# Loading and converting the input weights of a GLA + gated SSM kernel by column blocks, with the first group's projection moved into the second group's attention

## Chip, cores, metric

The kernel runs on one core of one Trainium2 chip. The metric is device time in microseconds for one launch; times of several runs are given by their median.

## What is computed

The first part is a gated linear attention over 4 batches, 8 heads, 768 steps and head size 48, in float32. The second part projects the attention's output, runs a linear recurrence, gates it and projects back. The weights `w_in` (384 x 1024), `w_out` (512 x 384) and `A_log` come as float64.

```python
for t in range(S):                       # q, k, v, alpha: (4, 8, 768, 48)
    state = alpha[:, :, t, :, None] * state + np.einsum('bhd,bhe->bhde', k[:, :, t], v[:, :, t])
    y[:, :, t] = np.einsum('bhd,bhde->bhe', q[:, :, t], state)
x = y.transpose(0, 2, 1, 3).reshape(B, S, H * D)          # (4, 768, 384)
val, gate = np.split(x @ w_in, 2, axis=-1)                # 512 columns each
for t in range(S):
    h = exp(A_log)[0] * h + val[:, t, :]
    ys[:, t, :] = h
out = (gate * sigmoid(gate) * ys) @ w_out
```

## The kernel before

**Groups.** Each batch is cut into three groups of 256 steps, so there are 12 groups, numbered m or n. A group has two chunks of 128 steps. The work of a group has two halves: attention (m) and the projection part (n), which runs one group behind.

**Attention.** `natural_alpha` (L551) transposes alpha on PE and ACT copies it into `aT`. `products` (L586) is DVE's chain of running products: `first`, the scan `prod`, the scan `inv`. `natural_qk` (L559) transposes k and q, and its `times` multiplies them by the products into `Z`. That is the form of groups 0 to 2, which are loaded in natural layout in 192-byte packets (`load_natural`, L417); later groups are loaded by `load_raw` (L396) in pieces of 32 partitions and turned by DVE. `scores` (L638) multiplies k and q on PE. `masks` (L648) copies one half of the scores by ACT and masks it on POOL, and masks the other half on DVE. `keys` (L629) transposes k, `state` (L679) adds the chunk's keys times values into a PSUM tile and has ACT copy it to `S_sb`, `values` (L655) and `carried` (L667) build y. `join` (L690) has ACT copy y into `xT` and then issues six small DMAs that move its last rows into place, for groups 0 and 1 from POOL's queue, later from those of SP and ACT.

**Projection.** `project(n, cc)` (L704) computes 128 of the 512 value columns (`pv`) and 128 of the gate columns (`pg`), six matmuls each; `gated` (L717) is a DVE scan over `pv`, a Silu on ACT over `pg` and a product on POOL into `f`. `output` (L728) is 16 matmuls with `w_out`, two ACT copies and two stores from SP. The tiles `pv`, `pg`, `o`, `tn` of alpha, `tp` and the warm-up tile share three PSUM buffers (`ps_mm`).

**Weights.** The float64 bits are loaded as pairs of 32-bit words into `bits_in` and `bits_out`. `load_w_in(half, engine)` (L440) loads one half of the partitions (0 to 63 or 64 to 127) in two DMAs, of 48 and of 16 rows, in 8-KB packets. `convert(i)` (L497) turns words into float32 for 128 value and 128 gate columns of `w_in` (i from 0 to 3) or for two row blocks of `w_out` (i = 4, 5): ACT scales the low words into `wr` (two buffers), DVE does two bit operations on the high words, and POOL adds (it is returned as a function, so that it can be called later).

**Order.** Every engine runs its instructions in the order in which the program text issues them. In the opening the load queue on SP holds, in this order: alpha, k, q of group 0, alpha of 1, v of 0, k and q of 1, the first half of `w_in`, v of 1, `w_out`, then alpha, k, q of group 2. The second half of `w_in` is issued from ACT's queue after `masks(0)`. The attention of groups 0 and 1 is written out (L768 to L832), with all four `convert` calls for `w_in` after `masks(1)` and before `state(1, 0)`. `warm` (L780) issues matmuls whose result nothing reads. Then the loop (L836) has for each n: project and gate four blocks, and between them the attention of n + 1 and the DVE steps (`go`) of group n + 2. For n = 0 there is no attention in it; instead it holds the alpha transposes of group 2 and the two conversions of `w_out`.

## Time and profile before

| | |
|---|---|
| median of 8 runs | 324.01 us (322.45 to 327.69) |
| profiled execution | 327.07 us |
| its span, first to last instruction | 325.3 us |
| PE busy | 294.0 us (90%), mean granted clock 0.961 |
| DVE busy | 227.2 us (70%) |
| POOL busy | 115.6 us (36%) |
| ACT busy | 97.1 us (30%) |
| first matmul of the projection of group 0 | 54.69 us |
| first matmul of the projection of group 1 | 80.96 us |
| first conversion of `w_in` (ACT, behind its last load) | 43.88 us |

Busy shares are means over the whole span. The two rows on the projections divide it into an opening, in which groups 0 and 1 are loaded, the weights come in and the first projection runs, and a loop of eleven rounds. A chain of waits follows the work that ended last back to what released it; a hole in a timeline stands in square brackets, with what ended it.

### The profile page before, as it was taken

What the parts mean: (1) busy time and instruction counts of PE and PEld (TensorE: products, weight loads), DVE (VectorE), ACT (ScalarE), POOL (GpSimd) and SP (SyncE); (2) the same over time, 40 slices, a digit from 0 to 9 for tenths busy, and PEclk for the clock granted to TensorE, in tenths of its full rate; (3) what the DMA queues carried; (4) which work ended last, traced back from release to release, by engine and by line L of the source; (5) the groups of instructions that cost most, each with busy time, mean ns of one, the idle gap of its engine ahead of it and who ended that gap; (6) DMA issues with size and microseconds to landing.
All of it is one profiled execution on the core that took longest, in us unless ns stands there. A gap on an engine that the chain in (4) does not pass through costs nothing.

```text
span 325.3 us, 5980 instructions
## 1 busy us (share of the span) xinstructions
PE 294.0 (90%) x2349; PEld 233.6 (72%) x2349; DVE 227.2 (70%) x244; ACT 97.1 (30%) x200; POOL 115.6 (36%) x109
## 2 busy tenths in 40 slices
PE   3998146969999999999999999999999999999991
PEld 3585145846886887878868878878688688786870
DVE  3857056493896896898998998989979689432110
ACT  4160233421421424224214324241243143221201
POOL 6033327490350610822704216318033054150020
PEclk9999856986999999999999999999999999999999
DMA  9999999951952955927919729559169220100101
GB/s 134 163 158 164 125 262 171 222 73 46 230 103 81 236 82 140 215 39 187 190 37 240 118 81 234 83 146 217 28 171 206 63 50 10 52 2 14 48 5 55
DMA packets 66029, 39.71 MB, mean 122 GB/s; under 512 B 47044, under 2 KB 65096, under 8 KB 65608
## 3 DMA queue, kind: packets, MB, share of 16 engines
q1 hardware_dynamic: 63376, 36.78, 58.7%
q10 hardware_dynamic: 2232, 2.27, 4.3%
q0 software_dynamic: 384, 0.20, 0.5%
q8 instruction: 20, 0.33, 0.5%
q14 instruction: 17, 0.14, 0.2%
HBM read 33.33 MB, written 4.72 MB: 117 GB/s over the span
## 4 chain that ended last, share of the span: by engine, by line
PE 80%; DMA 9%; DVE 3%; POOL 3%; ACT 2%; issue 0%; ACTq 0%; DVEq 0%; POOLq 0%
PE pv L713 21%; PE o L734 20%; PE pg L713 18%; DMA bits_in<-in_moe_w_in_dram 8%; PE sc L645 7%; PE y L664 5%; PE y L675 3%; PE st L685 3%; PE tp L635 2%; DMA a_log<-in_moe_A_log_dram 1%; POOL w_in L515 1%; POOL w_out L515 1%; ACT wr L510 1%; DVE inv L611 1%; DVE prod L599 1%; DVE Z L573 1%
## 5 line engine op out<-in xcount | busy, mean ns | idle before, releaser
L726 POOL TENSOR_TENSOR f<-sg,hh 128x256 f32<-128x256 f32 x48 | 60.6, 1262 | 145.7 <-ACT sg L725 144.2
L713 PE MATMUL pv<-xT,w_in 128*128 128x256 f32 x288 | 73.6, 392 | 0.0
L713 PE MATMUL pg<-xT,w_in 128*128 128x256 f32 x288 | 70.2, 380 | 0.0
L734 PE MATMUL o<-w_out,f 128*128 128x384 f32 x192 | 67.4, 505 | 2.9 <-POOL w_out L515 2.9
L713 PEld LDWEIGHTS pv<-xT,w_in 128*128 128x128 f32 x288 | 53.6, 193 | 12.1 <-issue 2.2
L713 PEld LDWEIGHTS pg<-xT,w_in 128*128 128x128 f32 x288 | 55.0, 191 | 7.6
L734 PEld LDWEIGHTS o<-w_out,f 128*128 128x128 f32 x192 | 37.7, 198 | 28.0 <-POOL w_out L515 3.9
L725 ACT ACTIVATE sg<-pg 128x256 f32<-128x256 f32 x48 | 18.4, 384 | 102.4 <-PE pg L713 89.6
L720 DVE TENSOR_TENSOR_SCAN hh<-a_dec,hh,pv 128x256 f32<-128x256 f32 x32 | 23.5, 733 | 33.5 <-PE pv L713 31.6
L652 POOL TENSOR_TENSOR A<-A,mask 128x512 f32<-128x512 f32 x24 | 30.0, 1269 | 35.1 <-ACT A L651 35.1
L599 DVE TENSOR_TENSOR_SCAN prod<-aT,first 128x1024 f32<-128x1024 f32 x12 | 32.8, 2736 | 0.1
L611 DVE TENSOR_TENSOR_SCAN inv<-aT,last 128x1025 f32<-128x1025 f32 x12 | 29.4, 2450 | 0.4
L738 ACT ACTIVATE o_sb<-o 128x384 f32<-128x384 f32 x24 | 11.8, 491 | 55.2 <-PE o L734 55.2
L645 PE MATMUL sc<-Z 48*128 48x128 f32 x384 | 25.5, 278 | 1.4 <-issue 0.8
L685 PE MATMUL st<-v,ktm 128*64 128x48 f32 x320 | 13.9, 232 | 14.0 <-DMA v<-in_v_dram 10.5
L645 PEld LDWEIGHTS sc<-Z 48*128 48x128 f32 x384 | 22.8, 188 | 5.0 <-issue 3.0
L685 PEld LDWEIGHTS st<-v,ktm 128*64 128x64 f32 x320 | 12.2, 146 | 17.8 <-issue 14.1
L664 PE MATMUL y<-A,v 128*64 128x128 f32 x384 | 24.7, 283 | 0.0
L720 DVE TENSOR_TENSOR_SCAN hh<-a_dec,pv 128x256 f32<-128x256 f32 x16 | 10.9, 681 | 16.4 <-PE pv L713 16.4
L664 PEld LDWEIGHTS y<-A,v 128*64 128x64 f32 x384 | 22.1, 143 | 0.2 <-issue 0.2
L653 DVE TENSOR_TENSOR A<-sc,mask 128x512 f32<-128x512 f32 x24 | 16.6, 691 | 7.9 <-PE sc L645 5.5
L590 DVE STREAM_TRANSPOSE aT<-raw_a 128x1024 f32<-128x1024 f32 x9 | 18.4, 2043 | 0.0
(86 smaller groups left out, 278.0 us busy)
## 6 DMA issues: line engine op xcount, KB each, us to landing
raw_k<-in_k_dram SPq DMA_DIRECT2D x24, 192.0 KB, 5.3
raw_q<-in_q_dram SPq DMA_DIRECT2D x24, 192.0 KB, 6.0
v<-in_v_dram SPq DMA_DIRECT2D x24, 192.0 KB, 4.5
out_dram<-o_sb SPq DMA_DIRECT2D x24, 192.0 KB, 1.9
raw_a<-in_alpha_dram SPq DMA_DIRECT2D x23, 192.0 KB, 4.0
raw_a<-in_alpha_dram SPq DMA_DIRECT2D x18, 176.0 KB, 4.1
raw_k<-in_k_dram SPq DMA_DIRECT2D x18, 176.0 KB, 5.5
raw_q<-in_q_dram SPq DMA_DIRECT2D x18, 176.0 KB, 4.9
```

Of the source, the lines that this page charges most:

```text
L590: nc.vector.transpose(out=to.rearrange("p h (c j) -> p h j c", j=NT), in_=raw_bufs[m % NR][name].rearrange("p h (j d) -> p h j d", d=D)[:, ...
L599: nc.vector.tensor_tensor_scan(out=prod, data0=aT[:, 0:4 * GC], data1=first.rearrange("p h n -> p (h n)"), initial=0.0, op0=ALU.mult, op1= ...
L611: nc.vector.tensor_tensor_scan(out=inv[:, ::-1], data0=aT[:, ::-1], data1=last.rearrange("p h n -> p (h n)")[:, 0:4 * GC + 1][:, ::-1], in ...
L645: nc.tensor.matmul(sc[i][:, p, :], Z[rows, p, 1, cols], Z[rows, p, 0, cols], start=True, stop=True)
L652: nc.gpsimd.tensor_mul(A[:, 1], A[:, 1], mb)
L664: nc.tensor.matmul(ys[m][i][ds(64 * s, 64), e, ds(c * C, C)], v_sb[:, c, 2 * p + i, :], A[:, i, p, :], start=(c == 0 and e == 0), stop=Fal ...
L685: nc.tensor.matmul(st[ds(64 * i, 64), p, :], ktms[c][:, p, i, :], vs[m % NV][:, c, 2 * p + i, 0:D], start=(ch == 0 and p == 0), stop=(ch = ...
L713: nc.tensor.matmul(pj, w_in[:, kk, vg, ds(cc * C, C)], xT[:, kk, :], start=(kk == 0), stop=(kk == NK - 1))
L720: nc.vector.tensor_tensor_scan(out=hh, data0=a_dec[:, cc:cc + 1].to_broadcast([C, GC]), data1=pv, initial=prev_h[cc][:, GC - 1:GC] if g el ...
L725: nc.scalar.activation(sg, pg, AF.Silu)
L726: nc.gpsimd.tensor_mul(fs[n][:, cc, :], sg, hh)
L734: nc.tensor.matmul(os[c], fs[n][:, cc, ds(c * C, C)], w_out[:, cc, :], start=(cc == 0), stop=(cc == NI - 1))
```

## The change

`load_w_in` now takes a block number i: it loads the 128 value and the 128 gate columns that `convert(i)` needs, for both halves of the partitions, in eight DMAs of 48 or 16 rows with packets of 1 KB. All four blocks are issued from SP, after v of group 1. `wr` has four buffers. `convert(0)` stands before `scores(1)`, `convert(1)` after `keys(1)`, `convert(2)` before `join(1)`, `convert(3)` before the second block of the projection; `masks(1)` stands ahead of `keys(1)`. Block 0 of the projection of group 0 runs between `convert(1)` and `state(1, 0)`, the other three after `join(1)`, and with them the round n = 0 leaves the loop and is written out. In the start, the Exp table is loaded by a first small activation, three warm calls and the alpha transposes come ahead of the transpose of `a_log`, and the Silu table is loaded after `scores(0)`.

```diff
--- before.py
+++ after.py
@@ -385,6 +385,7 @@
     p1 = pool("p1", 1)
     p2 = pool("p2", 2)
     p3 = pool("p3", 3)
+    p4 = pool("p4", 4)
     ps_sc = pool("ps_sc", 2, space=PS)
     ps_st = pool("ps_st", 1, space=PS)
     ps_mm = pool("ps_mm", 3, space=PS)
@@ -437,12 +438,18 @@
     bits_in = const.tile([C, NK, 2 * DI, 2], U32, name="bits_in")
     bits_out = const.tile([C, NI, DM, 2], U32, name="bits_out")
 
-    def load_w_in(half, engine):
-
-        for row, size, first, step in ((64 * half, D, 4 * half * D, D), (64 * half + D, R, (4 * half + 3) * D, R)):
-            engine.dma_start(out=bits_in[ds(row, size)].rearrange("p kk n two -> p kk (n two)"),
-                             in_=moe_w_in.bitcast(U32)[ds(first, NK * step)]
-                             .rearrange("(kk p) n -> p kk n", p=step)[0:size])
+    def load_w_in(i, engine):
+
+        for first_row, size in ((0, D), (D, R)):
+            for vg in range(2):
+                for s in range(2):
+                    row, step = (4 * s * D, D) if size == D else ((4 * s + 3) * D, R)
+                    cols = ds(2 * (vg * DI + i * C), 2 * C)
+                    engine.dma_start(
+                        out=bits_in[ds(64 * s + first_row, size), :, ds(vg * DI + i * C, C)]
+                        .rearrange("p kk n two -> p kk (n two)"),
+                        in_=moe_w_in.bitcast(U32)[ds(row, NK * step), cols]
+                        .rearrange("(kk p) n -> p kk n", p=step)[0:size])
 
     def load_w_out(i, engine):
         engine.dma_start(out=bits_out[:, ds(2 * i, 2)].rearrange("p cc n two -> p cc (n two)"),
@@ -505,7 +512,7 @@
             bits, w = bits_out[:, rows, None], w_out[:, rows, None, :]
         lo, hi = bits[..., 0], bits[..., 1]
         _, x, y, z = w.shape
-        r = p2.tile([C, x, y, z], I32, tag="wr", name="wr")
+        r = p4.tile([C, x, y, z], I32, tag="wr", name="wr")
         t = w.bitcast(U32)
         nc.scalar.activation(r, lo, AF.Copy, scale=2.0 ** -29)
         nc.vector.tensor_scalar(out=t, in0=hi, scalar1=3, scalar2=0x3FFFFFFF,
@@ -693,9 +700,12 @@
         xT = xTs[m] = p2.tile([C, 4, GC], FP32, tag="xT", name="xT")
         nc.scalar.activation(xT[:, 1::2], y[1], AF.Copy)
         nc.scalar.activation(xT[:, 0::2], y[0], AF.Copy)
-        for s in range(2):
-            for a in range(NK):
-                engines[s].dma_start(out=xT[ds(64 * s + D, R), a], in_=xT[ds(64 * s + R * a, R), 3])
+
+        def transfers():
+            for s in range(2):
+                for a in range(NK):
+                    engines[s].dma_start(out=xT[ds(64 * s + D, R), a], in_=xT[ds(64 * s + R * a, R), 3])
+        return transfers
 
 
     prev_h = [None] * NI
@@ -758,30 +768,31 @@
     load_v(0, SP)
     pair("k", 1, SP, SP)
     pair("q", 1, SP, SP)
-    load_w_in(0, SP)
     load_v(1, SP)
+    for i in range(NI):
+        load_w_in(i, SP)
     for i in range(2):
         load_w_out(i, SP)
 
     constants()
-
+    def warm(count):
+
+        t = ps_mm.tile([C, 4, C], FP32, tag="mm", name="warm")
+        for _ in range(count):
+            nc.tensor.matmul(t, ident, ident[:, None, :].to_broadcast([C, 4, C]), start=True, stop=True)
+
+    nc.scalar.activation(ok[:, 0:1], minus, AF.Exp)
+    warm(3)
+
+
+    natural_alpha(0)
     al = ps_mm.tile([C, NI], FP32, tag="mm", name="al")
     nc.tensor.transpose(al, a_log, ident[0:NI, 0:NI])
     nc.scalar.activation(a_dec, al, AF.Exp)
-    nc.scalar.activation(ok, start_p, AF.Silu)
-
-
-    natural_alpha(0)
     check_alpha(0)
     k_times, q_times = natural_qk(0, "k"), natural_qk(0, "q")
     for name in "akq":
         pair(name, 2, SP, SP)
-
-    def warm(count):
-
-        t = ps_mm.tile([C, 4, C], FP32, tag="mm", name="warm")
-        for _ in range(count):
-            nc.tensor.matmul(t, ident, ident[:, None, :].to_broadcast([C, 4, C]), start=True, stop=True)
 
     warm(5)
     for _ in products(0):
@@ -791,9 +802,9 @@
         q_times(c)
     for c in range(G):
         scores(0, c)
+    nc.scalar.activation(ok[:, 0:1], minus, AF.Silu)
     for c in range(G):
         masks(0, c)
-    load_w_in(1, ACT)
     for c in range(G):
         keys(0, c)
     natural_alpha(1)
@@ -806,7 +817,7 @@
     values(0, 1)
     state(0, 1)
     carried(0, 1)
-    join(0, (nc.gpsimd, nc.gpsimd))
+    join(0, (nc.gpsimd, nc.gpsimd))()
     k_times, q_times = natural_qk(1, "k"), natural_qk(1, "q")
     warm(4)
     for _ in steps:
@@ -814,29 +825,54 @@
     for c in range(G):
         k_times(c)
         q_times(c)
+    convert(0)()
 
     for c in range(G):
         scores(1, c)
     for c in range(G):
+        masks(1, c)
+    for c in range(G):
         keys(1, c)
-    for c in range(G):
-        masks(1, c)
-    for i in range(NI):
-        convert(i)()
+    convert(1)()
+    pj = project(0, 0)
+    gated(0, 0, *pj)
     state(1, 0)
     values(1, 0)
     values(1, 1)
     state(1, 1)
     carried(1, 0)
     carried(1, 1)
-    join(1, (nc.gpsimd, nc.gpsimd))
+    convert(2)()
+    join(1, (nc.gpsimd, nc.gpsimd))()
+    sums = convert(3)
+    pj = project(0, 1)
+    gated(0, 1, *pj)
+    sums()
+    sums = convert(NI)
+    pj = project(0, 2)
+    gated(0, 2, *pj)
+    sums()
+    natural_alpha(2)
+    sums = convert(NI + 1)
+    pj = project(0, 3)
+    gated(0, 3, *pj)
+    sums()
+    check_alpha(2)
+    loads(3)
+    load_v(2, SP)
+    for _ in products(2):
+        pass
+    output(0)
+    k_times, q_times = natural_qk(2, "k"), natural_qk(2, "q")
+    for c in range(G):
+        k_times(c)
+        q_times(c)
 
     checks = itertools.chain.from_iterable(check_w(i) for i in range(NW))
     value = None
-    for n in range(N):
+    for n in range(1, N):
         m = n + 1
-        att = 0 < n < N - 1
-        nat = n + 2 < NAT
+        att = m < N
         steps = products(n + 2) if n + 2 < N else iter(())
 
         def go(count):
@@ -849,36 +885,24 @@
         if n + 2 < N:
             load_v(n + 2, SP)
 
-        def attend():
+
+        pj = project(n, 0)
+        gated(n, 0, *pj)
+        if att:
             for c in range(G):
                 keys(m, c)
             for c in range(G):
                 scores(m, c)
-
-
-        pj = project(n, 0)
-        gated(n, 0, *pj)
-        if att:
-            attend()
-        if not nat:
-            go(1)
+        go(1)
         if att:
             for c in range(G):
                 masks(m, c)
         pj = project(n, 1)
         gated(n, 1, *pj)
-        if nat:
-            natural_alpha(n + 2)
-            check_alpha(n + 2)
-            convert(NI)()
-        else:
-            go(1)
+        go(1)
         pj = project(n, 2)
         gated(n, 2, *pj)
-        if nat:
-            convert(NI + 1)()
-        else:
-            go(2)
+        go(2)
         if att:
             state(m, 0)
             values(m, 0)
@@ -886,7 +910,7 @@
             state(m, 1)
             carried(m, 0)
             carried(m, 1)
-            join(m, (SP, ACT))
+            join(m, (SP, ACT))()
         pj = project(n, 3)
         gated(n, 3, *pj)
         go(10)
@@ -898,11 +922,6 @@
         if n == N - 1:
             value = nc.values_load(flag[0:1, 0:1], min_val=0, max_val=1)
         output(n)
-        if nat:
-            k_times, q_times = natural_qk(n + 2, "k"), natural_qk(n + 2, "q")
-            for c in range(G):
-                k_times(c)
-                q_times(c)
     return value
 
 
```

## The prediction

> **What bounds the kernel now.** I read the page, then the chain of waits in order of time, the timelines of PE, DVE, ACT and POOL up to 105 us, stage windows with the granted clock, and the DMA view in narrow windows. From 81 us on each group takes 22.17 or 22.61 us with PE busy all the time, and the change leaves that loop alone. The opening differs:
>
> ```profile
> 0.00:10.00 10.00, 4.32 (x21) 4.30 (x21) 3.99 (x12) 4.94 (x8) 5.21 (x19) 1.00 1.17 139
> 34.00:38.00 4.00, 0.00 (x0) 0.00 (x0) 0.00 (x0) 1.38 (x3) 2.48 (x2) 0.93 1.05 149
> 38.00:42.00 4.00, 0.00 (x0) 0.00 (x0) 0.00 (x0) 0.00 (x0) 0.00 (x0) 0.50 1.09 89
> 42.00:46.00 4.00, 1.75 (x25) 1.78 (x27) 2.02 (x4) 1.73 (x2) 0.39 (x1) 0.50 1.15 263
> 102.85:125.02 22.17, 22.17 (x185) 17.95 (x185) 18.28 (x17) 7.45 (x16) 6.90 (x6) 1.00 0.69 143
> ```
>
> After the stretch come PE, PE weight load, DVE, ACT and POOL busy us, then PE's clock, DMA share and GB/s. For 8 us no engine has work while DMA is full. Adding up the stages to 81 us, PE is busy 56.7 us, so 24.3 us are empty; this is where anything can be won. PE's timeline names the holes, and the chain what fills them:
>
> ```profile
> 32.62 1.09 PE L635 MATMUL tp<-ident,Z 128*128 128x128 f32 x8
> 44.25 1.10 PE L685 MATMUL st<-v,ktm 128*64 128x48 f32 x16 [10.53 <-DMA v<-in_v_dram]
> 51.78 1.10 PE L685 MATMUL st<-v,ktm 128*64 128x48 f32 x16 [3.48 <-ACT S_sb L688]
> 72.19 7.18 PE L734 MATMUL o<-w_out,f 128*128 128x384 f32 x12 [2.86 <-POOL w_out L515]
> ...
> 18.60 25.11 DMA bits_in<-in_moe_w_in_dram
> 43.88 1.73 ACT wr L510 x2
> 45.61 2.00 POOL w_in L515
> ```
>
> PE stands 10.5 us for v(1), queued behind the first half of w_in; then 3.5 us because ACT's S_sb copy stands behind four conversions whose bits landed only at 43.9; then for w_out. Two idle stretches halve the clock; the output at 72 us takes 7.18 us for 12 matmuls, where 16 take 5.16 us later.
>
> The DMA rate by packet (windows 10:12, 20:26, 26:32, 44:48, 58:64):
>
> ```profile
> DMA packets 1728, 0.33 MB, mean 164 GB/s; under 512 B 1728, under 2 KB 1728, under 8 KB 1728
> DMA packets 97, 0.78 MB, mean 130 GB/s; under 512 B 2, under 2 KB 2, under 8 KB 2
> DMA packets 169, 1.04 MB, mean 174 GB/s; under 512 B 43, under 2 KB 43, under 8 KB 43
> DMA packets 704, 1.49 MB, mean 374 GB/s; under 512 B 230, under 2 KB 230, under 8 KB 704
> DMA packets 1127, 1.33 MB, mean 221 GB/s; under 512 B 199, under 2 KB 1127, under 8 KB 1127
> ```
>
> 192-byte loads run at 164 GB/s, 48 rows of one half of w_in at 130, both halves in flight at 174, w_out over 128 partitions at 374 (384 within 46:48), the 32-partition loads at 221.
>
> [...]half a w_in is slow, both are faster, 128 rows are fastest. [...]L513 takes 0.96 us alone and 2.44 beside a POOL add.[...]
>
> **The changes, step by step.** Times below are of the new kernel unless marked; the sum is against the profiled 327.07 us (span 325.3).
>
> *Start.* The Exp table (1.28 us) loads before alpha lands, and al moves behind natural_alpha(0). Before, aT's copy at 7.55 stood behind two table loads and ok. Three warm calls start with ident, at 1.4; ten such matmuls took 4.46 us at full clock, so six take 2.7, or 5.4 at the half speed PE shows at first (8 transposes in 1.76 us against 0.87 later). They end near 6.0 and so may delay the transposes by 0.2, but those then run fast: first moves from 8.79 to about 7.8. From the ACT queue two DMA issues (0.33 and 0.44) leave, ahead of keys(0), which stood idle 0.27. The Silu table loads in ACT's idle stretch (7.66 before). Gain on the DVE chain: 1.1; bounds 0 (warm too long) and 1.6. Z(1) ends at 28.2 instead of 29.29; warm(4) lets scores(1) go at 28.5.
>
> *Transfers.* v(1) leads: 2048 packets at 864 per us, from 18.5 to 20.9. w_in is now 32 issues on SP (was 2 there and 2 on ACT). At 0.44 and 0.33 each they cost SP 12.4 us; behind them stand w_out and the loads of group 2, paced by DMA anyway. The rate of 3.15 MB in 1-KB packets is the unknown. A 48-row piece alternates between halves every 144 KB, nine packets per engine: 130 if the engines go in step, 174 or some 200 if pieces of both halves overlap, 221 at best from the 32-partition row. I take 170: 18.5 us, and with 1 us to report (my estimate; a 16-KB xT transfer takes 1.8 in all) blocks land at 26.5, 31.1, 35.8 and 40.4; w_out at 384 by 42.5 and 44.5; alpha(2) at 46.9.
>
> *Attention with conversions.* convert(0): DVE 28.2 to 29.75 (0.55 + 0.96), POOL add (1.99) to 31.7. Scores take 3.1 to 31.6, keys 0.9 to 32.5. Masks on POOL (2 by 1.25) now follow the add, to 34.2[...]. project(0,0) needs xT(0): its POOL DMAs are issued from 24.2; the second join took about 8.1 from first issue to last packet, so 32.8. It ends at 35.4; its gating scan stands behind convert(1), to 35.7. state, values, state, carried: 3.7, to 39.1. That takes 6.6 us of PE under the stream. convert(2) holds POOL from 39.3 (ACT's wr is behind S_sb) to 41.3, the six xT issues (6 by 0.5) to 44.3.
>
> *POOL's queue is what is late next.* project(0,1) ends at 41.7, project(0,2) at 44.3 (pg waits for a PSUM buffer until the scan behind convert(3), 42.6, so hidden). POOL: f1 to 45.0, add(3) to 47.0, f2 to 47.7, first w_out add to 49.7. PE idles 44.3 to 46.9 for alpha(2). project(0,3) needs add(3): 47.8 to 50.4. f3 to 51.5, then the last w_out add, between 2.0 and 3.78 us as in the old trace[...]: 53.5 to 55.3. output(0) gets two matmuls in and then waits 2.4 to 4.2 us; its rest costs 4.5 at full clock and up to 6.3 with the clock halved; transposes 1.75. Group 1 starts between 59.7 and 63.3. I take 62.5, near the slow end, since the two gaps invite the half clock. Before, the same point was 80.96. **Sum:** 80.96 - 62.5 = 18.5 us less, 1.1 of it from the start. 327.07 becomes 308.6; the profile is 3 us above the median of 324.01, so for medians 305.5.
>
> Four wr buffers instead of two take away ACT's wait of 4.0 us, off the path now. Moving masks ahead of keys costs nothing: PE's keys need only Z. Group 3's loads need not be late: after alpha(2), two 192-byte loads (4.7), then 2.2 MB at 221 (10) and v(2) (2.4) end near 64, while v(2) is used 10.5 us into the new group. If that cover were gone, each microsecond late would count.
>
> **Rivals.** *Stream in step:* [...]120 to 131 GB/s. At 120 w_in ends 7.7 us later, the last block delays scan 1, add(3) and alpha(2), and group 1 starts near 69: 12 us gained, 312. For it: 130 in the old trace with the same 48 rows[...]. *Stream fast and clock full:* 215 or more, last add 2.0 us, PE throughout at full speed; scores to transposes hold 26 us of PE work, so 54.5 is the floor and 58 likely: 23 us gained, 301. For it: the 221 row; against: POOL's queue. *Slower:* 1-KB pieces at an 8-KB pitch, all engines at the same column offset, land far below any row seen. Each microsecond of w_in beyond 26 goes to the path; the 12 us are used up at 38 us, or 82 GB/s. At half the old rate, 65 GB/s, it is 48.4 us: 22 later, 10 us lost, 334. For it: no such packets in the trace, and even 8-KB packets ran at 130; against: 1408-byte packets at 221. A *no change* result needs 79 to 88 GB/s. *The change doesn't do what it says:* waits of convert(0) could cover all of w_in; then DVE and PE hold from 28 to 40 and about 9 us remain of the gain. I leave this inside the range.
>
> **How the numbers follow.** Forecast 0.52 (its own range 302 to 309), stream in step or waits too wide 0.21, fast 0.15, no change 0.03, slower 0.09. Range 299 to 315: it takes in forecast, most of the slow stream and of the fast one. A measurement tells about 1% (3.2 us) from no change; faster by more 0.88, within 0.03, slower 0.09.
>
> **What would show it.** Right: no PE wait for v at all; the w_in window at 140 to 200 GB/s, ended by 41; pv of group 0 near 33, beside unlanded blocks; output(0) waiting on POOL L515; a loop of 22.2 us from about 62. Wrong: under 100 GB/s between 21 and 40 us; project(0,0) waiting for xT; PE idle at v(2) or alpha of group 3 after 62; a loop longer than 22.6.

## The result, and the profile after

| | before | after |
|---|---|---|
| median, same session | 324.96 us (321.40 to 327.69, 56 runs) | 327.10 us (325.11 to 330.71, 19 runs) |
| ratio | | 1.0093, interval 1.0068 to 1.0117 |
| profiled execution, span | 327.07 us, 325.3 us | 325.08 us, 323.3 us |
| first matmul of group 1's projection | 80.96 us | 76.33 us |
| start of output(1) and of output(2) | 97.53, 119.70 us | 92.89, 118.36 us |

The medians say 0.9% slower, with an interval clear of 1; the forecast was 305.5 us. The two profiled executions stand the other way round from the medians, because the one of before was among its slowest and the one of after among its quickest; so stages are compared here, not spans.

First the stage windows of the changed kernel, with the columns of before:

```profile
34.00:38.00 4.00, 0.00 (x0) 0.00 (x0) 0.00 (x0) 0.00 (x0) 0.00 (x0) 0.64 0.86 197
38.00:42.00 4.00, 0.00 (x0) 0.00 (x0) 2.90 (x5) 2.94 (x6) 1.23 (x1) 0.50 0.99 306
42.00:46.00 4.00, 3.37 (x8) 2.74 (x9) 3.31 (x3) 0.71 (x1) 4.00 (x3) 0.50 1.32 236
118.36:140.97 22.61, 22.61 (x201) 18.39 (x200) 18.06 (x18) 7.45 (x16) 8.99 (x6) 1.00 0.64 141
```

There is still a stretch in which no engine works, and the clock still falls to 0.50. From output(2) on the loop is as before: 22.61 us for a group, PE busy throughout. The timelines of PE, DVE and ACT name what the stretch waits for:

```profile
30.06 1.09 PE L642 MATMUL tp<-ident,Z 128*128 128x128 f32 x8
42.63 2.93 PE L723 MATMUL pv<-xT,w_in 128*128 128x256 f32 x6 [11.48 <-POOL w_in L522]
45.35 2.77 PE L723 MATMUL pg<-xT,w_in 128*128 128x256 f32 x6
...
68.91 5.83 PE L744 MATMUL o<-w_out,f 128*128 128x384 f32 x12 [4.32 <-POOL w_out L522]
```

```profile
39.06 0.56 DVE L518 TENSOR_SCALAR w_in<-bits_in 128x768 uint32<-128x768 uint32 x1 [11.20 <-DMA bits_in<-in_moe_w_in_dram]
```

```profile
39.06 0.91 ACT L517 ACTIVATE wr<-bits_in 128x768 int32<-128x768 uint32 x1 [15.50 <-DMA bits_in<-in_moe_w_in_dram]
```

v(1) is no longer waited for. In its place convert(0), which needs the first quarter of `w_in` (its last packet passed at 25.3 us), starts at 39.06, behind the last packet of the fourth quarter (38.2). The first projection stands 11.48 us for it and then runs at half clock: 2.93 and 2.77 us for two sets of six matmuls that take 1.56 and 1.46 later.

The second loss lies between output(1) and output(2), and was not there before. PE's timeline after the change and before it:

```profile
92.89 5.32 PE L744 MATMUL o<-w_out,f 128*128 128x384 f32 x16
101.27 1.53 PE L723 MATMUL pv<-xT,w_in 128*128 128x256 f32 x6 [3.06 <-issue]
```

```profile
97.53 5.32 PE L734 MATMUL o<-w_out,f 128*128 128x384 f32 x16
102.69 1.46 PE L713 MATMUL pv<-xT,w_in 128*128 128x256 f32 x6
```

After the change, the chain of waits from 90 us on, a line of SP's waits (total us, how often, longest), and SP's timeline (its DMA issues; the 77.71 line is four loads of k, the 93.34 line four of q):

```profile
91.48 0.59 ACTq L707
...
92.11 0.59 ACTq L707
...
92.74 1.80 DMA xT<-xT
```

```profile
SPq L406 <- DMA xT<-xT: 13.1, 3, 12.5
```

```profile
77.71 3.06 SPq L406 DMA_DIRECT2D raw_k<-in_k_dram  x4
93.34 2.00 SPq L406 DMA_DIRECT2D raw_q<-in_q_dram  x4
95.39 1.20 SPq L430 DMA_DIRECT2D v<-in_v_dram  x2
96.90 2.71 SPq L707 DMA_DIRECT2D xT<-xT  x3
```

And before, in the same place:

```profile
82.34 1.79 SPq L405 DMA_DIRECT2D raw_k<-in_k_dram  x4
84.24 4.76 SPq L405 DMA_DIRECT2D raw_q<-in_q_dram  x4
...
98.02 1.87 SPq L698 DMA_DIRECT2D xT<-xT  x3
```

After the change SP issues k of group 4 and then stands 12.5 us before q of group 4, released by a DMA that moves `xT`; before it went straight on from k to q. (The row counts three waits: the first three loads of q wait for ACT's three transfers, one for each, and the first wait is the long one.) That is a transfer of group 2's join, issued from ACT's queue at 91.5; q of group 4 has nothing to do with it. SP's own three transfers of the same join stand behind q and v and go out at 96.90 instead of at once, and PE, done with output(1) at 98.2, starts again only at 101.27. The profile names no releaser for this hole ("issue"); the landing of SP's last transfer, issued at 99.0, fits it, and in a run below (the one with four more DMAs) the same hole reads `[3.70 <-DMA xT<-xT]`. Output(1) to output(2) takes 25.47 us; before it took 22.17. So of the 4.6 us that the opening gains in this pair of profiles, 3.3 go here.

### The profile page after: what moved, and what is told of

It reads as the page before. It is cut to its first block, busy times and chain, and to the rows that moved or that the text cites. A ratio compares the mean times of both kernels' runs of the same rounds, so it can differ in the third digit from the quotient of the medians.

```text
span 323.3 us, 6026 instructions
## 1 busy us (share of the span) xinstructions
PE 293.2 (91%) x2355; PEld 230.1 (71%) x2355; DVE 230.8 (71%) x244; ACT 97.0 (30%) x201; POOL 115.4 (36%) x109
## 4 chain that ended last, share of the span: by engine, by line
PE 77%; SPq 8%; DMA 5%; DVE 3%; POOL 2%; issue 2%; ACT 0%; ACTq 0%; POOLq 0%
PE pv L723 20%; PE pg L723 18%; PE o L744 18%; PE sc L652 6%; PE y L671 6%; DMA bits_in<-in_moe_w_in_dram 4%; SPq L421 4%; PE st L692 3%; PE y L682 3%; SPq L448 2%; PE tp L642 2%; DVE w_out L520 2%; SPq L430 1%; POOL w_out L522 1%; DMA raw_q<-in_q_dram 1%
## 5 line engine op out<-in xcount | busy, mean ns | idle before, releaser
L723 PE MATMUL pg<-xT,w_in 128*128 128x256 f32 x288 | 71.3, 384 | 0.0
L744 PE MATMUL o<-w_out,f 128*128 128x384 f32 x192 | 65.9, 497 | 4.3 <-POOL w_out L522 4.3
L744 PEld LDWEIGHTS o<-w_out,f 128*128 128x128 f32 x192 | 37.0, 194 | 28.5 <-POOL w_out L522 4.9
L659 POOL TENSOR_TENSOR A<-A,mask 128x512 f32<-128x512 f32 x24 | 31.0, 1312 | 27.6 <-ACT A L658 27.6
L652 PE MATMUL sc<-Z 48*128 48x128 f32 x384 | 24.7, 278 | 0.0
L671 PE MATMUL y<-A,v 128*64 128x128 f32 x384 | 23.4, 274 | 0.0
L671 PEld LDWEIGHTS y<-A,v 128*64 128x64 f32 x384 | 20.8, 137 | 0.2 <-issue 0.2
L597 DVE STREAM_TRANSPOSE Z<-raw_q 128x1024 f32<-128x1024 f32 x9 | 18.3, 2034 | 0.0
L597 DVE STREAM_TRANSPOSE Z<-raw_k 128x1024 f32<-128x1024 f32 x9 | 18.2, 2020 | 0.0
```

The costliest lines, as they stand in the source:

```text
L597: nc.vector.transpose(out=to.rearrange("p h (c j) -> p h j c", j=NT), in_=raw_bufs[m % NR][name].rearrange("p h (j d) -> p h j d", d=D)[:, ...
L652: nc.tensor.matmul(sc[i][:, p, :], Z[rows, p, 1, cols], Z[rows, p, 0, cols], start=True, stop=True)
L659: nc.gpsimd.tensor_mul(A[:, 1], A[:, 1], mb)
L671: nc.tensor.matmul(ys[m][i][ds(64 * s, 64), e, ds(c * C, C)], v_sb[:, c, 2 * p + i, :], A[:, i, p, :], start=(c == 0 and e == 0), stop=Fal ...
L723: nc.tensor.matmul(pj, w_in[:, kk, vg, ds(cc * C, C)], xT[:, kk, :], start=(kk == 0), stop=(kk == NK - 1))
L744: nc.tensor.matmul(os[c], fs[n][:, cc, ds(c * C, C)], w_out[:, cc, :], start=(cc == 0), stop=(cc == NI - 1))
```

## The experiments

Two theories went into them. *Wide wait:* convert(0) waits for all of `w_in`, because the 32 loads write one tile `bits_in`. In the program order (the list of each engine's instructions of this kernel, with the semaphores, counters that tell of finished work, that they wait on) its first instructions wait on all eight semaphores that the 32 loads use, each at the count that the last of the loads brings it to, and those of convert(1) to convert(3) wait on no load at all; in the trace the instructions with these waits run from 38.11 to 39.06 us. *Shared semaphores:* in the program order of this kernel, DMAs issued from SP and from ACT draw on one set of eight semaphores, which the build hands out, and a DMA waits for the one that had its semaphore before, whatever it moved and whoever issued it. In the trace the first q load of group 4 (SP, 93.34 us) has the semaphore of ACT's first transfer (91.48 us), number 106 in both. Rivals: the stream itself is late or slow, the POOL queue holds the first projection anyway, or SP stops because the transfers of one group go over two queues.

### Four tiles for the bits

```diff
-    bits_in = const.tile([C, NK, 2 * DI, 2], U32, name="bits_in")
+    bits_in = [const.tile([C, NK, 2, C, 2], U32, name=f"bits_in{i}") for i in range(NI)]
...
-                        out=bits_in[ds(64 * s + first_row, size), :, ds(vg * DI + i * C, C)]
+                        out=bits_in[i][ds(64 * s + first_row, size), :, vg]
...
-            bits = bits_in.rearrange("p kk (vg n) two -> p kk vg n two", vg=2)[:, :, :, ds(i * C, C)]
+            bits = bits_in[i]
```

> The changed kernel with bits_in as four tiles, one for each column block; every load, conversion and check else as in the changed kernel (the range check takes four pieces of 768 columns in place of three of 1024). Theory W: in the changed kernel the first reads of the one bits_in tile wait for all 32 loads (39.06 us), so the blocks are not converted as they land. With four tiles convert(0) starts at 27 to 28 us, project(0,0) near 33 in place of 42.63, no half clock before 48 us, group 1 near 63 to 67 in place of 76.33, and 9 to 13 us less in all: 314 to 318. Rival D: the blocks themselves are late (the load of the first is not complete before 38): no change, 326 to 328.

316.43 us (4 runs, 315.72 to 316.79), ratio to before 0.9752 (0.9676 to 0.9827). PE's timeline:

```profile
31.94 1.56 PE L723 MATMUL pv<-xT,w_in 128*128 128x256 f32 x6 [0.21 <-POOL w_in L522]
...
56.10 5.83 PE L744 MATMUL o<-w_out,f 128*128 128x384 f32 x12 [3.01 <-POOL w_out L522]
...
88.84 2.90 PE L723 MATMUL pv<-xT,w_in 128*128 128x256 f32 x6 [3.45 <-issue]
```

The loads, their packets and the order of work are those of the changed kernel; only the tile is cut (and with it the range check of the weights, four reads in place of three, late in the loop). In the program order each `convert` now waits at the counts of its own eight loads. The first projection starts at 31.94 instead of 42.63 (forecast 32.8) and group 1 at 63.51 (forecast 62.5). The wide wait is shown, and it cost 10.7 us. Why the build makes a read of a part wait for all (it may count the tile as a whole, or the address ranges of the blocks, which interleave) is not separated by this run. The stop behind output(1) is still there, at 88.84, and here the clock is halved behind it (0.51 from 87.8 to 94.7 us): output(1) to output(2) takes 28.74 us, 6.6 more than 22.17.

### Group 2's transfers all on SP

```diff
-            join(m, (SP, ACT))()
+            join(m, (SP, SP) if m == 2 else (SP, ACT))()
```

> The changed kernel with the last rows of xT of group 2 moved by six DMAs on SP in place of three on SP and three on ACT. Theory L: in the changed kernel SP stands 12.5 us before the third load of q of group 4, because it takes a DMA semaphore that ACT's xT transfer holds; behind it stand v of group 4 and SP's own xT transfers, and project(2,0) waits. Without ACT's three: no wait over 3 us on SP in front of that load, the round of group 1 takes 22 to 22.6 us in place of 24.9, and 2.5 to 3.5 us less: 323.5 to 325. Rival: the round is long for the loads of groups 3 and 4 (late transfers), and the three extra issues on SP cost 1.8 us: 327 to 329.

321.54 us (13 runs, 320.99 to 322.18), ratio 0.9911 (0.9878 to 0.9944), 5.6 us below the changed kernel. SP issues q of group 4 right behind k, and output(1) to output(2) is 22.17 us:

```profile
76.97 1.79 SPq L406 DMA_DIRECT2D raw_k<-in_k_dram  x4
78.87 2.02 SPq L406 DMA_DIRECT2D raw_q<-in_q_dram  x4
```

That is more than the 323.5 to 325 us expected, and more than the 3.3 us of the profile; the third profile of the changed kernel, below, shows a part of the difference (4.9 us). Against before, in the same session, 0.9% are now won. But the edit fits two reasons: it takes the transfers from ACT, and it also puts them on one queue.

### Why SP stops

Four more DMAs ahead of the loop turn every semaphore number by four, to those that SP's transfers have in the kernel before:

```diff
-        engine.dma_start(out=bits_out[:, ds(2 * i, 2)].rearrange("p cc n two -> p cc (n two)"),
-                         in_=moe_w_out.bitcast(U32)[ds(2 * C * i, 2 * C)].rearrange("(cc p) n -> p cc n", p=C))
+        for row, size in ((0, 64), (64, 32), (96, 32)):
+            engine.dma_start(out=bits_out[ds(row, size), ds(2 * i, 2)].rearrange("p cc n two -> p cc (n two)"),
+                             in_=moe_w_out.bitcast(U32)[ds(2 * C * i, 2 * C)]
+                             .rearrange("(cc p) n -> p cc n", p=C)[ds(row, size)])
```

> The changed kernel with each of the two w_out loads issued as three DMAs (64, 32 and 32 partitions) instead of one: four more DMAs on SP ahead of the loop, the same bytes, nothing else moved; group 2's transfers are split over SP and ACT as in the changed kernel. In the program order, SP's DMAs and ACT's draw on one set of eight semaphores in turn, and four more turn the assignment back to that of the kernel before, so that ACT's transfers of group 2 share a semaphore with SP's own transfers and not with the q load of group 4. Theory A (the changed number of DMAs moved that assignment, and SP's wait comes from it): SP's wait of 12.5 us for an xT transfer goes, the interval from output(1) to output(2) is 22.2 us again instead of 25.5 to 27.0, and the time falls to about 322 us. Theory B (the wait comes from two queues issuing the transfers, or from the new order of the opening, whatever the semaphores): the wait stays, interval above 25, time 326 to 328.

326.86 us (20 runs), ratio 1.0092 (1.0065 to 1.0120): nothing won. SP's timeline and a line of its waits:

```profile
77.96 3.15 SPq L406 DMA_DIRECT2D raw_k<-in_k_dram  x4
93.99 1.75 SPq L406 DMA_DIRECT2D raw_q<-in_q_dram  x4
```

```profile
SPq L406 <- DVE Z L631: 12.8, 1, 12.8
```

This expectation was wrong: output(1) to output(2) takes 27.79 us. The program order shows why: all numbers turned together, and ACT's first transfer still stands eight places ahead of q of group 4, between the alpha loads. In the kernel before it stands behind the first q load, and eight places on there is one of SP's own transfers, which comes after it anyway. It is the place in the hand-out that decides, not the number. (The row puts the wait down to DVE's Z. In the program order that load waits on DVE only for a memset of its buffer, done long before, and on ACT's transfer; Z's end, at 93.92, only fell next to the transfer's landing.)

So two more runs. One keeps two queues and takes away the sharing, since POOL's DMAs have semaphores of their own in this program (111 to 118 in the trace, none of which a DMA of SP or ACT uses); the other keeps the sharing and takes SP's transfers away:

```diff
-            join(m, (SP, ACT))()
+            join(m, (SP, nc.gpsimd) if m == 2 else (SP, ACT))()    # first run
+            join(m, (ACT, ACT) if m == 2 else (SP, ACT))()         # second run
```

> The changed kernel with group 2's second three xT transfers on POOL's queue instead of ACT's; SP keeps the first three, so two queues still issue them. POOL's DMAs draw on semaphores of their own, so in the program order SP's loads of group 4 take the eight numbers without a gap. Theory A (q of group 4 waits because it takes the number of an ACT transfer): SP's 12.5 us are gone, output(1) to output(2) is 22.2 to 24 us (POOL's three issues of 0.5 us delay its product f by 1.5), time 322 to 323. Theory B (two queues for one group's transfers, or the order of the opening): the stop stays, 326 to 328.

> The changed kernel with all six transfers of group 2 on ACT's queue, none on SP's. In the program order the first q load of group 4 still takes a number that an ACT transfer has. Theory A (shared numbers): SP stands before q of group 4 until the ACT transfer has landed near 93 us, although SP issues no transfer; but PE's next projection needs only ACT's six transfers (3.6 us), so the gap on PE is shorter than in the changed kernel: output(1) to output(2) 22.2 to 24 us. Theory B (SP stops because of the transfers in its own queue): q of group 4 is issued near 79 us, and the interval is about 22.2.

With POOL 322.04 us (20 runs), ratio 0.9934 (0.9911 to 0.9958), output(1) to output(2) 22.17 us and no stop. With ACT alone 329.15 us in its one execution. SP's timeline of the first; then, of the second, SP's timeline, SP's waits and PE's timeline:

```profile
80.34 2.06 SPq L406 DMA_DIRECT2D raw_q<-in_q_dram  x4
```

```profile
80.11 14.54 SPq L406 DMA_DIRECT2D raw_k<-in_k_dram  x4
96.28 2.31 SPq L406 DMA_DIRECT2D raw_q<-in_q_dram  x4
```

```profile
SPq L406 <- DMA xT<-xT: 24.2, 8, 12.7
```

```profile
115.70 5.32 PE L744 MATMUL o<-w_out,f 128*128 128x384 f32 x16
124.06 2.90 PE L723 MATMUL pv<-xT,w_in 128*128 128x256 f32 x6 [3.04 <-issue]
```

SP stands 12.7 us for a transfer of group 2 although it issues none of them itself, now already among the four loads of k, whose second has the number of ACT's first transfer. So two queues are not the reason (no stop with SP and POOL, 12.7 us with ACT alone), and all four edits agree with the shared semaphores. In the second run the interval to output(2) is only 23.0 us, as expected, but SP then stops again, 8.1 us before q of the next group, and its own transfers of group 3 go out late, at 119.50: output(2) to output(3) takes 28.9 us instead of 22.61, with half clock in it. The stop was moved on, not removed.

### Both edits together

> Both edits: four bits_in tiles and the six transfers of group 2 on SP. W and L together: 12 to 16 us under the changed kernel, 311 to 315, that is 10 to 14 under the kernel before. If only W holds, as with the tiles alone; if only L, as with the transfers alone; if POOL's queue binds behind the stream as the prediction had it, output(0) of group 0 waits 2.4 to 5 us for the last w_out add.

309.07 us (4 runs, 307.91 to 310.22), ratio 0.9518 (0.9443 to 0.9593), better than the 311 to 315 expected. With the stop gone, cutting the tile is worth 12.5 us (321.54 to 309.07). Group 1 starts at 65.10. What is left ahead of it, in the timelines of PE, DVE and POOL:

```profile
50.72 1.45 PE L744 MATMUL o<-w_out,f 128*128 128x384 f32 x4
57.09 6.42 PE L744 MATMUL o<-w_out,f 128*128 128x384 f32 x12 [4.92 <-POOL w_out L522]
```

```profile
45.23 5.61 DVE L518 TENSOR_SCALAR w_out<-bits_out 128x768 uint32<-128x768 uint32 x1 [0.33 <-DMA bits_out<-in_moe_w_out_dram]
```

```profile
46.16 1.80 POOL L522 TENSOR_TENSOR w_in<-w_in,wr 128x768 int32<-128x768 int32 x1
47.93 0.72 POOL L736 TENSOR_TENSOR f<-sg,hh 128x256 f32<-128x256 f32 x1
48.62 1.80 POOL L522 TENSOR_TENSOR w_out<-w_out,wr 128x768 int32<-128x768 int32 x1
52.58 0.72 POOL L736 TENSOR_TENSOR f<-sg,hh 128x256 f32<-128x256 f32 x1 [2.16 <-DVE first L603]
53.26 3.78 POOL L522 TENSOR_TENSOR w_out<-w_out,wr 128x768 int32<-128x768 int32 x1
```

The last `w_out` add ends at 57.0, output(0) has waited 4.92 us for it, and its clock is halved after that (0.50 from 57 to 61 us). The add itself takes 3.78 us beside DVE's scan, against 1.80 for the one at 48.62.

### The last w_out add ahead of f3

```diff
     pj = project(0, 3)
-    gated(0, 3, *pj)
     sums()
+    gated(0, 3, *pj)
```

> The kernel with four bit tiles and group 2's transfers all on SP, with POOL's last w_out add called before the gating of block 3 instead of after it, so that the add does not stand behind the product f3, which waits for scan and Silu. Theory A (the last w_out add in POOL's queue is what output(0) waits for, 4.92 us in the kernel with both edits): the add starts 1.5 to 2.5 us earlier, the wait falls by as much, and f3 follows the add and becomes the next releaser, so 1 to 2.5 us are won: 306.5 to 308. Theory B (the add is bound by DVE's bit operations[...], not by its place in the queue): it ends at the same time within 0.5 us, and the median stays at 309 within 1 us.

303.67 us (4 runs, 303.47 to 304.54), ratio 0.9372 (0.9307 to 0.9437). The add no longer stands behind f3, which waits for projection, scan and Silu. The timelines of POOL and of PE:

```profile
50.91 1.81 POOL L522 TENSOR_TENSOR w_out<-w_out,wr 128x768 int32<-128x768 int32 x1 [0.96 <-DVE w_out L520]
52.67 0.73 POOL L736 TENSOR_TENSOR f<-sg,hh 128x256 f32<-128x256 f32 x1
```

```profile
51.38 5.52 PE L744 MATMUL o<-w_out,f 128*128 128x384 f32 x16
58.49 1.46 PE L723 MATMUL pv<-xT,w_in 128*128 128x256 f32 x6
```

Output(0) doesn't wait at all, runs at full clock, and group 1 starts at 58.49. More was won than the 1 to 2.5 us expected: 5.4 us between the medians, 4.7 by the two ratios. The add ends 4.3 us earlier, of which 2.35 are its earlier start and 1.97 its length, as it is out of the scan's way too (1.81 us instead of 3.78), and with the wait of 4.92 us the half clock goes: output(0) takes 5.52 us in all, where its two parts took 1.45 and 6.42. This version beats both kernels.

### The named parts by themselves

v(1) ahead of `w_in` in the kernel before:

```diff
-    load_w_in(0, SP)
     load_v(1, SP)
+    load_w_in(0, SP)
```

> The kernel before with one edit: v of group 1 is issued ahead of the first half of w_in. PE's longest wait, 10.5 us for v, goes. Theory S (the stream decides): state(1,0) and values(1) run at 33 us, but ACT's copy S_sb stands behind the four conversions, which land 2.4 us later than before, so nothing is won: same as before or up to 2.5 us more, 324 to 327.5. Rival V (the wait for v was on the path by itself): 5 to 10 us less, 315 to 320.

325.99 us (20 runs), ratio 0.9995 (0.9959 to 1.0031). State(1, 0) goes at 34.94 instead of 44.25, and PE then waits for S_sb, which stands on ACT behind the four conversions:

```profile
34.94 1.10 PE L685 MATMUL st<-v,ktm 128*64 128x48 f32 x16
...
50.94 1.10 PE L685 MATMUL st<-v,ktm 128*64 128x48 f32 x16 [11.52 <-ACT S_sb L688]
```

The largest hole of the old profile was thus worth nothing by itself. The new start (Exp table, three warm calls, order of the alpha transposes, Silu table) was tried in the kernel before, and taken out of the 303.67 us version:

```diff
+    nc.scalar.activation(ok[:, 0:1], minus, AF.Exp)
+    warm(3)
...
+    natural_alpha(0)
     al = ps_mm.tile([C, NI], FP32, tag="mm", name="al")
...
-    nc.scalar.activation(ok, start_p, AF.Silu)
-    natural_alpha(0)
...
+    nc.scalar.activation(ok[:, 0:1], minus, AF.Silu)
```

> The kernel before with the start edit alone: Exp table by a first small activation, three warm calls, the alpha transposes ahead of the transpose of a_log, Silu table after the scores of group 0. In the profile after, first starts at 7.45 us instead of 8.79. Theory A (the whole DVE chain up to the k and q products moves with it): Z(1) about 1.3 us earlier, but PE in the old order then waits for v(1), which is bound by DMA at 44 us, so the median stays within 0.5 us of before. Theory B (the prediction's 1.1 us counts in full on the time): 1.1 to 1.3 us less than before, also in the old order. A gain beyond 2 us, or a loss beyond 1, fits neither.

> The 303.67 kernel with the start as in the kernel before. The profiles so far put first of group 0 at 7.40 to 8.81 us with the new start, by whether the six warm matmuls take 4.24 or up to 5.49 us, and at 8.79 and 8.91 with the old one. Theory A (the start sets the second group's k and q products and through them everything up to group 1): 0.5 to 1.3 us more than 303.67. Theory B (later waits for alpha of group 2 and w_out, which are paced by DMA, absorb it): within 0.3 us of 303.67.

In the old order 324.71 us against 323.86, ratio 1.0025 (0.9999 to 1.0052): nothing. Taken out of the new order it costs 1.4 us by the medians (305.05, 304.70 to 305.54), a little over the expected 1.3. These are of two sessions; by the ratios to before (0.9389 and 0.9372) it is 0.6 us, and in the profiles output(1) comes 0.84 us later. So the same edit is hidden in the old order, while in the new one 0.6 to 1.4 us of it seem to reach the end. Its gain also differs from one execution to the next. PE's timelines of the old order with the new start, and of the changed kernel:

```profile
1.43 5.35 PE L772 MATMUL warm<-ident 128*128 128x512 f32 x6 [1.43 <-POOL ident masks.py:199]
```

```profile
1.43 4.28 PE L782 MATMUL warm<-ident 128*128 128x512 f32 x6 [1.43 <-POOL ident masks.py:199]
```

The alpha transposes follow these six matmuls, and `first` comes at 8.51 us in the one case and 7.45 in the other. In the changed kernel the clock records begin at 4.36 us, with the full clock; in the other run the six matmuls took 1.07 us longer, which puts its full clock near 6.5 us (an estimate: until then they go at about half speed, as six took 5.49 us in the kernel with both edits and ten 4.46 us later in the changed kernel). With the old start `first` came at 8.79 to 8.91 in every profile.

Last, block 0 of the first projection moved back behind join(1), once in the kernel with both edits and once in the 303.67 us version:

```diff
     convert(1)()
-    pj = project(0, 0)
-    gated(0, 0, *pj)
     state(1, 0)
...
     join(1, (nc.gpsimd, nc.gpsimd))()
+    pj = project(0, 0)
+    gated(0, 0, *pj)
     sums = convert(3)
```

> The kernel with four bit tiles and group 2's transfers all on SP, with block 0 of the first projection and its gating moved back from inside the second group's attention to after its join. Theory A (the prediction's: POOL's queue and the last w_out add set the start of output(0), not PE): the 2.6 us of PE work move from a stretch where PE waits to one where PE is again short of work; the last w_out add ends within 1 us of where it was, and the median is 0 to 1 us above the 309.07 of the kernel with both edits. Theory B (PE's work between 32 and 48 us is on the path, so that the early projection is worth its own length): 2.5 to 3.5 us above, about 312.

> The kernel with four bit tiles, group 2's transfers on SP and POOL's last w_out add ahead of f3 (303.67 us), and with block 0 of the first projection moved back behind the second group's join. The wait of output(0) for POOL is gone in the 303.67 kernel, so PE's work between 32 and 58 us has less slack. Theory A (alpha of group 2 and POOL's queue still leave 2 us or more of room on PE): within 1 us of 303.67. Theory B (with that wait gone the place of block 0 counts in full): about 2.6 us more, 306.3.

309.82 (309.34 to 310.26) beside 309.07, and 304.24 (303.92 to 304.62) beside 303.67: 0.6 to 0.75 us, with ranges that overlap, and in different sessions. The part that gave the change half its name moves hardly anything; PE has room there either way, as it stands for alpha of group 2 (2.33 us in the 303.67 us version).

### Each kernel profiled again

> The changed kernel, unaltered, profiled a second time. Its first profiled execution took 325.08 us, the median is 327.1, and that trace shows the round of group 1 at 24.9 us with the full clock granted. Theory A (SP's wait for an xT transfer empties PE long enough to halve its clock in most executions, and this is what separates the median from the first profile): about 327 us, with a clock of 0.5 for some us at 90 to 105 us and a round of group 1 of 26 to 28 us. Theory B (the rest is spread over the execution): about 327 us with full clock there and the round at 25.

> The kernel before, unaltered, profiled a second time. Its first profiled execution took 327.07 us with a mean clock of 0.961, while its median is near 324 to 325; executions near 322 have a mean clock of 0.97. Expected if this one is among the quick ones: group 1 starts near 76 to 77 us instead of 80.96, with full clock in the first projection or in output(0); if not, about 80 again. The loop after group 1 takes 244.3 us in both cases.

> The changed kernel, unaltered, profiled a third time. The two profiles so far (325.08 and 326.14 us) have a mean clock of 0.970 to 0.971, the executions near 328 to 329 have 0.961 to 0.964. If this execution is one of those, theory A (the stop for the xT transfer sometimes halves the clock) says a stretch of 5 to 7 us at 0.5 behind 100 us and a round of group 1 of 27 to 28 us; theory B (the lower clock sits in the opening) says a round of 25 us and a later start of group 1.

| execution | us | clock | output(1) | output(2) |
|---|---|---|---|---|
| before, first | 327.07 | 0.961 | 97.53 | 119.70 |
| before, second | 325.16 | 0.960 | 96.03 | 118.20 |
| after, first | 325.08 | 0.971 | 92.89 | 118.36 |
| after, second | 326.14 | 0.970 | 92.87 | 118.73 |
| after, third | 328.31 | 0.964 | 93.44 | 120.48 |

Output(1) starts 2.6 to 4.7 us earlier after the change, and output(1) to output(2) is 3.3, 3.7 and 4.9 us longer. The second execution had the full clock behind output(1), as its theory B said. PE's timeline of the third:

```profile
101.96 2.90 PE L723 MATMUL pv<-xT,w_in 128*128 128x256 f32 x6 [3.20 <-issue]
```

Here the stop has cost the clock as well, which the first execution (1.53 us for the same six matmuls) was spared. Both theories of that run hold a part: output(0) too lost 1.2 us to half clock (7.06 us for its last 12 matmuls instead of 5.83).

Why the one execution and not the other can be read from the clock records in the traces. In the first profile of each kernel every stretch between two changes of the clock is a whole number of steps of 3.41 us (before: 8, 3, 1, 2, 4, 2 and 72; after: 9, 4, 6, 1 and 73), on a grid that stands elsewhere in each execution: after the change the clock is halved at 35.08 us in the first execution and at 101.46 in the third, 19.4 steps later. The gap on the grid of the third execution, then on that of the first (behind the stretch and its length comes PE's busy time; PE's clock is the third number from the end):

```profile
98.05:101.46 3.41, 0.71 (x3) 0.09 (x1) 0.00 (x0) 0.98 (x2) 0.00 (x0) 1.00 1.16 164
101.46:104.88 3.42, 2.92 (x7) 2.41 (x8) 0.00 (x0) 0.00 (x0) 0.00 (x0) 0.50 1.01 258
```

```profile
96.53:99.94 3.41, 1.69 (x6) 0.67 (x4) 0.34 (x1) 0.98 (x2) 0.00 (x0) 1.00 1.31 184
99.94:103.35 3.41, 2.08 (x10) 1.88 (x11) 0.43 (x1) 0.00 (x0) 0.00 (x0) 1.00 0.80 233
```

In the third execution nearly the whole gap falls into one step, and the step after it has half clock. In the first it is split over two steps, each with work in it, and the clock stays. So it does in the second (1.00 from 98 to 108 us), although its gap (3.45 us) is longer than that of the third (3.20): its two steps hold about 1.7 us of work each. In the first profiles of both kernels, from the first record on, each step at full clock with no PE work, or with 0.31 us of it (after), 0.64 or 1.19 us (before), was followed by half clock, as was the one with 0.71 us in the third execution; those with 1.45 us or more were not. That is no limit: in the run with v(1) first about 2.3 us of work stand in the 3.41 us before 33.0 us, and the eight matmuls that start at 33.04 then take 1.97 us, against 1.09 in the kernel before.

The results list the clock of every execution. After the change there are three groups: six with 0.970 or more take 325.1 to 326.5 us, eight with 0.964 to 0.968 take 326.5 to 328.4, and seven with 0.961 or 0.962 take 327.8 to 330.7. One step at half clock is 0.005 of the mean (half of 3.41 us in 325), so the groups are about one such step apart. With the stop removed (all transfers on SP) all 13 lie between 0.969 and 0.973 and within 1.2 us. The median of after is thus a mixture, and one profile shows only one kind; where the steps lie in the executions that were not profiled isn't shown. The second execution of before was near its median and starts group 1 at 79.46 us, about where it was expected for such a one. A quick one of before (321.4) was not caught, so where those save their 3 us stays open.

## Why the prediction was wrong

What held:

- *Transfers.* 3.15 MB between 20.4 and 38.2 us are 177 GB/s (taken: 170). The last packets of the four blocks passed at 25.3, 29.5, 34.1 and 38.2 us; with the prediction's 1 us to report (its author's estimate) taken off, the forecast was 25.5, 30.1, 34.8 and 39.4. Here the 1-KB packets, in pieces that alternate between partition halves, were thus as fast as the 8-KB packets of both halves before (174), and the slower rival had no ground. SP's 32 issues took 18.8 us and not 12.4 (18.0 to 36.9, alongside the stream).
- *Start.* 1.1 forecast; `first` moved by 1.3 in the first profile, but that is luck in part: over ten profiles with the new start it came between 7.40 us, where the six warm matmuls took 4.24 us, and 8.81, where they took 5.49, and at 8.79 to 8.91 with the old.
- *POOL's queue.* With the wide wait gone, project(0,0) starts at 31.94 (32.8), alpha of group 2 is there at 46.06 (46.9), output(0) waits 3.0 to 4.9 us for the last `w_out` add (2.4 to 4.2), which ends near 56 and at 57.0 (53.5 to 55.3), and group 1 starts at 63.5 to 65.1 (62.5). With both waits gone the kernel takes 309.07 us, inside the given range.
- *A reading that does not hold.* "For 8 us no engine has work": the line of 34 to 38 us shows ACT busy for 1.38 and POOL for 2.48 us. POOL ends at 37.45, and nothing runs for 6.4 us from there. The sum goes by PE and is not touched.

What failed, as two steps:

- *Attention with conversions: "convert(0): DVE 28.2 to 29.75".* It took the wait of a conversion to be for its own block. It was for all 32 loads, to 39.06. The prediction had this as a rival, "the change doesn't do what it says", with "about 9 us remain of the gain. I leave this inside the range". Both its price and its place were too kind. In one session, before took 325.11 us, the kernel with both waits gone 309.07 and the one with the wide wait alone 321.54: the gain without it is 16.0 us instead of 18.5, and the wide wait takes 12.5 of it instead of 9.5. So 3.6 us were left, not 9, since the first projection came at 42.63, at half clock, with all of the POOL queue behind it. The rival belonged in the chances as a case of its own: the one tile that all loads write stood in the code, and the width of the wait in the program order.
- *"From 81 us on ... the change leaves that loop alone" and "Group 3's loads need not be late".* The loop's code is indeed untouched, and the data of group 3 were in time. But SP's DMAs in the loop share semaphores with ACT's transfers, and where those come in the hand-out moved with the opening. That costs 3.3 to 4.9 us in the three profiles and 5.1 to 5.6 between medians of different sessions (327.10 against the 322.04 and 321.54 of the two kernels without the stop), which is more than the rest of the gain; so the kernel became slower. "A loop longer than 22.6" stood among the signs of being wrong, and came; but no rival had a wait in the loop. The one on the other side, a stream under 82 GB/s, looked for the loss in the wrong place.

The fast rival ("54.5 is the floor and 58 likely: 23 us gained, 301") named the limit that stands once POOL's last add is moved: group 1 at 58.49, 303.67 us. There the stream ran at the forecast rate, so it was not the transfer but the order of two POOL instructions that stood in between.

## What to carry to other kernels

Cutting a load into pieces started the first consumer earlier only when the dependence was cut as well: with one tile convert(0) went at 39.06 us, with a tile for each piece at 26.75. So give each piece a tile of its own, or read in the program order what the consumer waits for before counting the gain. A DMA on one queue waited 12.5 us for one on another with the same completion semaphore, so a change to the opening stopped a loop whose code it didn't touch; look in the waits of the issuing engine for a DMA released by a transfer it has nothing to do with. A stall of 3.20 us on PE cost more than itself, as the clock was halved behind it (2.90 us for six matmuls instead of 1.53), and one of 3.45 us in another execution of the same kernel did not: it hung here on where the stall fell on a grid of 3.41 us that differs between executions. So compare intervals between fixed points over several profiles before believing a span.

## What the runs showed of the hardware that was not expected

- A DMA on SP stood 12.5 us for a 16-KB transfer that ACT had issued, only because the build had given the two the same semaphore (106 in the trace of the changed kernel); with the transfer on POOL, under a semaphore of its own, the stop was gone.
- A VectorE bit operation, 0.56 us elsewhere, took 5.61 us, from 45.23 to 50.84, while POOL ran f, an add, f and an add back to back (45.48 to 50.42): the one VectorE instruction lasted until four on POOL had finished. In the changed kernel another one, 0.96 us elsewhere, took 5.84.
- After 3.0 to 3.5 us without matmuls the clock was full in some executions of a kernel and 0.50 in others, and the longer gap was not the one that halved it (3.45 us did not, 3.20 did); what differed was the place of the gap on the grid of 3.41-us steps. The step ahead of the half clock did not have to be idle: it held 0.71 us of PE work in the third execution of the changed kernel, and 1.02 us in the kernel with four tiles (53.71 to 57.12), where the 12 matmuls of output(0) then took 5.83 us.
- The six warm matmuls at the start took between 4.24 and 5.49 us from the same starting time, 1.43 us: 4.26 and 4.28 in two executions of the changed kernel, 5.49 in the kernel with both edits, where the eight transposes behind them took 1.24 us instead of 1.04 as well.
